# DeltaNet attention into a SiLU MLP: odd heads' copies and moves first, outputs stored in bundles, MLP steps and V's loads placed anew

## The chip, the core and the metric

The kernel runs on one core of a Trainium2 chip. Its time is the device time in microseconds (us). The core's engines are TensorE (PE; its weight loads are PEld), VectorE (DVE), ScalarE (ACT), GpSimd (POOL) and SyncE (SP), whose queue issues nearly all DMAs here. Each engine works through its own instructions in order; they wait for each other by semaphores.

## The reference

For 4 batches and 8 heads, over 768 tokens of 48 elements, a delta rule runs from token to token; its output, laid out as 3072 rows of 384, goes through an MLP with 2048 hidden units.

```python
k_n = k / (np.linalg.norm(k, axis=-1, keepdims=True) + 1e-06)
for t in range(S):
    kt, vt, bt = (k_n[:, :, t], v[:, :, t], beta[:, :, t, None])
    y[:, :, t] = np.einsum('bhd,bhde->bhe', q[:, :, t], state)
    v_old = np.einsum('bhde,bhd->bhe', state, kt)
    state = state + bt[:, :, :, None] * np.einsum('bhd,bhe->bhde', kt, vt - v_old)
...
x = y.transpose(0, 2, 1, 3).reshape(B * S, H * D)
h = x @ w_in
out = (h * (1.0 / (1.0 + np.exp(-h)))) @ w_out
```

## The kernel before

**Chunks.** The 768 tokens are cut into six chunks of 128 (c = 0 to 5), each into two halves of 64 tokens (hf = 0, 1). Batches come in two groups of two (g = 0, 1). Inside a chunk the delta rule is a triangular system per head. Its inverse is made in 32x32 blocks: `prepare` makes the scores of the next chunk on TensorE (`score`, L514) and sends their diagonal blocks to DRAM and back (`block_out`, `block_in`: "blocks", "g"), so that each of the 128 partitions holds one block. `invert` (L614) solves them on VectorE in 31 steps of two instructions (L625, L630), then scales the result (L633) and sends it out ("low", "up") and in again ("xe", "xi", "crossed").

**One chunk's solve** (L970) is a fixed chain on TensorE with evacuations between: merge (L780, into py), keys (L826), second merge (L780, into px), then for each half: inner products and old outputs together (L838, L904), `made` = update of the state (L858) and new outputs (L917), and between the halves keys again. `made` (L954) ends with `copy_out`, which runs `even_heads` (L925) for group 0; the next step of `solve` runs it for group 1 and then `move`.

**The way into the MLP.** `even_heads` copies the odd heads' rows of the output bank into "part" (one copy of 48x512), then the even heads' rows straight into xT (six copies). The odd heads' rows need other partitions, so five DMAs per half (`move`, L895; out L897) take them from "part" to xT, for both groups together. In chunk 1's first half group 1's copies are VectorE's (`by_dve`), else all are ScalarE's.

**The MLP** of a half is `feed_forward` (L1205), a chain of 30 steps: `hidden` (L1032) has 16, of three matmuls each (128x256 moving), with a SiLU on ScalarE after every second; `combine` (L1132) has 14, of four matmuls (128x192), in seven chains of eight matmuls. `combine` works with sums of weights and of hidden values, which VectorE makes (`sum_g`, L1128; the first sums of the three groups of hidden values stand at hidden steps 10 and 16 and at the first combine step). It writes the output tile "o" (one buffer) from the fourth combine step on (L1170, L1173, L1176 on ScalarE, L1157 on VectorE) and stores it at its end (`store`, L1057: four DMAs of 96 KB). Chunk 0's MLP uses `project` (L1062) instead, with eight bundles of projection matmuls (L1074) that lie beside chunk 1's solve. Every matmul stands in the trace as two records: a hidden step is 6 records, a combine step 8.

**The order of the work** is written out by hand. `pin` keeps each engine in program order, and `in_line` (L92) keeps SP's DMAs in order. A string per chunk (`chunks`, L1479) says what comes next: "s" one step of `solve`, "r" one step of the MLP (any pending chunk's), "y" one step of `prepare`, "g" the start of the next inversion, "i" one inversion step, "k" the loads of K, "m" a step of the key lengths. The string at L1543 does it for chunk 0 and the start of chunk 1 ("t" is a sum of weights, L1110, "z" a scaling of V, "f" a narrowing step of a weight, L229 to L249, "c" ends the projection). SP's order follows from that: in `solve`, `load_v(c + 1)` (L1013; eight DMAs, L198) stands behind the second half's inner products, `follow` loads the next q in blocks (twelve DMAs, L162).

Of the kernel before, what the change touches and what calls it, by code (L numbers as in the profile page):

```python
# [19 lines left out]
def kernel(  # L20
# [12 lines left out]
    DM, DFF = moe_w_in.shape  # L33
# [78 lines left out]
    def together(*parts):  # L112
        for _ in zip_longest(*parts):
            pass
# [223 lines left out]
    xis = [xi[:, g] for g in range(2)]  # L338
    crossed = const.tile([P, HH, T], FP32, name="crossed")

    def busy(n=1, after=None, how=NoSync):

        for _ in range(n):
            pw = bank(CC, "pw")
            done = pin(nc.tensor.matmul(
                pw[:, 0:DM], lhsT=ident[:],
                rhs=states[0][:].rearrange("p u a w -> p (u a w)")[:, 0:DM], start=True, stop=True,
            ))
            tensor.append(done.ins.engine)
            if after is not None:  # L350
                behind(done, after, how)
                after = None
# [572 lines left out]
    def even_heads(c, g, hf, py):  # L925

        xT, half = x_half(c, g, hf)
        if g == 0:
            parts[c, hf] = work.tile([P, 2, NP, C], FP32, name="part", tag="x", bufs=1)
        part = parts[c, hf][:, g]  # L930
        by = by_dve if c == 1 and hf == 0 and g == 1 else by_act
        by(part[0:D], py[0:D].rearrange("p (a t) -> p a t", a=NP))
        for h in chained(range(1, H, 2), range(0, H, 2)):
            f = D * h
            while f < D * (h + 1):
                n, at = min(D * (h + 1) - f, P - f % P), W * (1 - h % 2) + f - D * h
# [12 lines left out]
        yield  # L949
# [4 lines left out]
    def made(c, hf):  # L954

        together(update(c, 0, hf), update(c, 1, hf))
        together(new(c, 0, hf), new(c, 1, hf))
        copy_out()

    def follow(c):  # L960
# [9 lines left out]
    def solve(c):  # L970
# [31 lines left out]
        for hf in range(2):  # L1002
            if hf == 1:
                together(keys(c, 0, 1), keys(c, 1, 1))
                if c > 1:
                    follow(c)
                yield
            for g in range(2):
                together(inner(c, g, hf), old(c, g, hf))
            if hf == 1:  # L1010
                if c == 1:
                    follow(c)
                load_v(c + 1)  # L1013
            yield
            made(c, hf)
            yield
            copy_out()
            move()
            if hf == 0:
                yield  # L1020
# [11 lines left out]
    def hidden(c, hf):  # L1032

        for f in range(NFF // 2):
# [19 lines left out]
                    sum_g(which, f // FG - 1)  # L1054
            yield

    def store(c, hf, o, n, cols=slice(0, DM), two_queues=False):  # L1057
        for u in range(HB):
            row = (n * HB + u) * S + c * C + hf * W
            issue(out[row : row + W, cols], o[W * u : W * (u + 1), n, cols], two_queues and u == 1)  # L1060

    def project():  # L1062
# [6 lines left out]
        for f in range(NFF):  # L1069
            assert ("out", f // 2) in narrowed  # L1070
            for i in range(2 * HB):
                hf, n = i // HB, i % HB
                at = (f % 2) * GT + n * C
                pin(nc.tensor.matmul(  # L1074
                    pos[i][:, 0:DM], lhsT=hidden_of(0, hf, f // 2)[:, at : at + C],
                    rhs=w_outs[f // HFF][:, f % HFF, :], start=(f == 0), stop=(f == NFF - 1),
                ))
                if f == NFF - 1:
                    to = (o, rest)[hf]
                    pin(nc.scalar.mul(to[:, n], pos[i][:, 0:DM], 0.5))  # L1080
                    store(0, hf, to, n)
                if n == HB - 1 and (f < NFF - 1 or hf == 0):
                    yield
        A.append(rooms[0])
# [46 lines left out]

    def combine(c, hf):  # L1132

        o = mlp.tile([P, 2, DM], FP32, name="o", bufs=1)
        kept = mlp.tile([P, 3, HM], FP32, name="kept", bufs=1)
        px, py = bank(M, "px"), bank(M, "py")
# [61 lines left out]
        keep(2, py[:, left])  # L1198
        add(o[:, 0, right], kept[:, 2])
        add(o[:, 0, left], kept[:, 0])  # L1200
        for n in range(2):
            store(c, hf, o, n)
        yield

    def feed_forward(c, hf):  # L1205
# [220 lines left out]
    def prepare(c):  # L1426
# [50 lines left out]
    sums_made = sum_w()  # L1477
    later = {}
    chunks = {  # L1479
# [5 lines left out]
    }  # L1485

    def script(text):

        nonlocal pieces
        for word in text.split():  # L1490
# [25 lines left out]
                paced(load_q, 1)  # L1516
            elif what == "o":
                busy(n)
            elif what == "h":
                size_half(1, pins[seen_on])  # L1520
            elif what == "v":
# [6 lines left out]
                later["inv"] = invert(1, step)  # L1528
            elif what == "i":
                go(later["inv"], n)  # L1530
            elif what == "z":
                size(1, sizes_1.pop(0))
            elif what == "t":
# [6 lines left out]
                pieces = chained(feed_forward(1, 0), feed_forward(1, 1))  # L1540

    for text in (
        "s f3 s q q s j4 b j36 r j4 f j16 q f j4 f j16 r j44 b j4 q j4 r f r j22 f j12 f j8 f b j8 f j8 r j16 e r f j99 h f r f2 l s l r l p r l f p l s l2 f r3 l3 p l s l3 p l2 r l f l4 f l f l3 p l s l2 s2 f r f r p l3 g i p l p f i p f l i r3 i r v f i2 r3 i2 r i r i3 b r2 f2 r2 i r2 i2 r2 i f b i r i3 f2 r2 f r3 f i2 r f i f r3 f r f i f r i2 r i2 k i2 b r2 i r i r z r i r s r b z s b r2 t r2 f s r2 t2 m2 t2 b m f r m s f b r m r m2 b m f s r s m4 c s m7 r t s m r m5 s r m2 t2",  # L1543
    ):
        script(text)
    for c in range(1, NCH):
# [5 lines left out]
        for word in chunks[c].split():  # L1552
# [9 lines left out]
                inverse = invert(c + 1, step)  # L1562
            elif what == "i":
                go(inverse, n)
            elif what == "k":
                load_k(c + 2)
                if in_blocks(c + 2):
# [37 lines left out]
```

## Time and profile before

| | us |
|---|---|
| median of three runs | 650.05 |
| lowest and highest of them | 647.34, 651.13 |
| the profiled execution, its own time | 648.18 |
| span of that execution, first to last instruction | 646.2 |
| TensorE busy in it | 624.3 |
| VectorE, ScalarE, GpSimd busy | 398.0, 214.3, 91.0 |

The mean granted TensorE clock of that execution was 0.989. The profile is one execution; its time stands 1.87 us below the median. "Busy" counts an engine's instructions from start to end as the profile shows them; matmuls are pipelined and their ends modelled. An idle time is written with what ended it: "<-DMA xT<-part" means that the instruction waited for the DMA that writes xT from part; "issue" that the profile names nothing.

### The profile page before, as it was taken

The numbers are of one execution on the slowest core, as the hardware profiler recorded it, in microseconds if no ns is written. First come the engines' busy times: TensorE is split into PE (matmuls) and PEld (weight loads), VectorE is DVE, ScalarE is ACT, GpSimd is POOL, SyncE is SP. The second block draws the span as 40 slices with busy tenths as digits, with TensorE's granted clock in tenths as the row PEclk, the third lists the DMA queues.
The fourth block names the chain that finished last, engine by engine and source line by source line (L and its number), as shares of the span: only waits on it lengthen the run. The fifth ranks groups of instructions, "written<-read, shape, count | busy, mean of one in ns | idle before, by whom it ended". The sixth has DMA issues, their size and how long they took to land.

```text
span 646.2 us, 21378 instructions
## 1 busy us (share of the span) xinstructions
PE 624.3 (97%) x9406; PEld 546.1 (85%) x9406; DVE 398.0 (62%) x911; ACT 214.3 (33%) x497; POOL 91.0 (14%) x92
## 2 busy tenths in 40 slices
PE   7789999999999999999999999999999999999997
PEld 5478788666789988989988989989989989789997
DVE  5776889989765974554975454976454973102112
ACT  2456673441441122451122451122451122441111
POOL 5023721336020020010020010020011000000000
PEclk9969999999999999999999999999999999999999
DMA  9955833440479251359142259333163024100101
GB/s 138 212 144 174 257 81 88 116 81 3 98 133 156 52 91 19 84 113 160 39 91 36 66 121 160 57 78 45 38 144 71 20 66 50 40 13 1 25 0 25
DMA packets 145676, 54.70 MB, mean 85 GB/s; under 512 B 117152, under 2 KB 138912, under 8 KB 145584
## 3 DMA queue, kind: packets, MB, share of 16 engines
q1 hardware_dynamic: 143136, 52.93, 40.1%
q8 instruction: 74, 1.21, 0.8%
q10 hardware_dynamic: 2448, 0.41, 0.4%
q14 instruction: 18, 0.15, 0.1%
HBM read 40.14 MB, written 11.01 MB: 79 GB/s over the span
## 4 chain that ended last, share of the span: by engine, by line
PE 76%; DVE 11%; DMA 7%; SPq 2%; issue 2%; ACT 1%; ACTq 0%; POOL 0%; DVEq 0%; POOLq 0%
PE phid L1039 30%; PE px L1146 13%; PE py L1146 10%; PE po L1074 5%; DVE rank L625 4%; DVE x L630 3%; PE pb_c L838 3%; PE pa L527 2%; PE pb_c L826 2%; PE pb_c L1074 2%; PE pyc L917 1%; PE pb_c L858 1%; DMA up<-x 1%; DVE sums_of_g L1128 1%; PE pyc L904 1%
## 5 line engine op out<-in xcount | busy, mean ns | idle before, releaser
L1039 PE MATMUL phid<-xT,w_in 128*128 128x256 f32 x1152 | 258.4, 382 | 2.6 <-DMA xT<-part 1.3
L1039 PEld LDWEIGHTS phid<-xT,w_in 128*128 128x128 f32 x1152 | 215.9, 190 | 34.3 <-issue 4.3
L1049 ACT ACTIVATE gT<-phid 128x512 f32<-128x512 f32 x88 | 52.6, 597 | 144.8 <-PE phid L1039 131.5
L625 DVE SCALAR_TENSOR_TENSOR rank<-g,step,x 128x31 f32<-128x31 f32 (+15 forms) x124 | 49.7, 401 | 37.5 <-DMA g<-blocks 34.1
L1128 DVE TENSOR_TENSOR sums_of_g<-gT 128x384 f32<-128x384 f32 (+1 forms) x60 | 31.1, 538 | 57.3 <-ACT gT L1049 46.6
L1146 PE MATMUL py<-w_out,sums_of_g 128*128 128x192 f32 x320 | 56.8, 329 | 0.0
L1146 PE MATMUL px<-sums_of_w,sums_of_g 128*128 128x192 f32 x320 | 56.8, 329 | 0.0
L1146 PEld LDWEIGHTS px<-sums_of_w,sums_of_g 128*128 128x128 f32 x320 | 52.2, 190 | 0.5
L1146 PEld LDWEIGHTS py<-w_out,sums_of_g 128*128 128x128 f32 x320 | 52.2, 190 | 0.4
L630 DVE TENSOR_TENSOR x<-x,rank 128x31 f32<-128x31 f32 (+15 forms) x124 | 42.5, 343 | 4.3
L465 POOL TENSOR_TENSOR vf<-vf,n_slot 128x768 f32<-128x768 f32 x10 | 15.0, 1508 | 171.4 <-DMA vf<-in_v_dram 125.6
L486 DVE STREAM_TRANSPOSE kq<-stage 128x512 f32<-128x512 f32 x28 | 28.4, 1109 | 10.1 <-DMA stage<-in_q_dram 10.1
L542 ACT COPY xT<-pyc 48x128 f32<-48x128 f32 (+2 forms) x126 | 32.7, 260 | 1.6
L1146 PE MATMUL px<-sums_of_w,gT 128*128 128x192 f32 x160 | 28.4, 329 | 0.0
L1146 PE MATMUL py<-w_out,gT 128*128 128x192 f32 x160 | 28.4, 329 | 0.0
L1146 PE MATMUL px<-w_out,gT 128*128 128x192 f32 x160 | 28.0, 327 | 0.0
L1146 PEld LDWEIGHTS px<-w_out,gT 128*128 128x128 f32 x160 | 26.4, 190 | 0.5
L838 PEld LDWEIGHTS pb_c<-vf,xi 64*64 64x64 f32 x736 | 23.5, 138 | 4.0 <-issue 3.7
L548 POOL COPY g<-x 64x256 f32<-64x256 f32 x4 | 5.0, 1239 | 151.8 <-DVE x L633 151.8
L1146 PEld LDWEIGHTS py<-w_out,gT 128*128 128x128 f32 x160 | 26.1, 190 | 0.3
L1146 PEld LDWEIGHTS px<-sums_of_w,gT 128*128 128x128 f32 x160 | 26.1, 190 | 0.2
L1157 DVE TENSOR_TENSOR o<-o,kept 128x192 f32<-128x192 f32 (+1 forms) x29 | 11.5, 421 | 24.0 <-ACT kept L1154 24.0
(221 smaller groups left out, 920.7 us busy)
## 6 DMA issues: line engine op xcount, KB each, us to landing
vf<-in_v_dram SPq DMA_DIRECT2D x48, 96.0 KB, 3.0
out_dram<-o SPq DMA_DIRECT2D x42, 96.0 KB, 2.2
w_out<-in_moe_w_in_dram SPq DMA_DIRECT2D x4, 768.0 KB, 4.4
sums_of_w<-in_moe_w_out_dram SPq DMA_DIRECT2D x4, 768.0 KB, 4.5
blocks<-ap SPq DMA_DIRECT2D x44, 64.0 KB, 1.9
g<-blocks SPq DMA_DIRECT2D x5, 512.0 KB, 3.5
kb<-in_k_dram SPq DMA_DIRECT2D x12, 192.0 KB, 4.8
kb<-in_k_dram SPq DMA_DIRECT2D x24, 96.0 KB, 4.4
```

Of the source, the lines that this page charges most:

```text
L465: pin(nc.gpsimd.tensor_tensor(out=vf, in0=vf, in1=of, op=ALU.mult))
L486: pin(nc.vector.transpose(out=kqs[c, b][:, :, j, :].rearrange("p a (i m) -> p a m i", i=T), in_=src.rearrange("p a (m d) -> p a m d", d=D) ...
L527: pin(nc.tensor.matmul(pa[e][half, p * n * W : (p + 1) * n * W], lhsT=kq[rows, p, 0, half], rhs=kq[rows, p, js[0] : js[-1] + 1, half], sta ...
L542: return pin(nc.scalar.copy(to, of))
L625: pin(nc.vector.scalar_tensor_tensor(out=tv, in0=g[:, 0:m, m : m + 1].to_broadcast([P, m, n]), scalar=step[:, m : m + 1], in1=x[:, m : m + ...
L630: yield pin(nc.vector.tensor_tensor(out=x[:, 0:m, m:T], in0=x[:, 0:m, m:T], in1=tv, op=ALU.add))
L838: yield pin(nc.tensor.matmul(pz[rows, n * D : (n + 1) * D], lhsT=xis[g][rows, u * H + 2 * p + e, :], rhs=vfs[c][rows, hf, g * HB + u, p, : ...
L1039: pin(nc.tensor.matmul(ph[:, j * GT : (j + 1) * GT], lhsT=w_in[:, a, (2 * f + j) * P : (2 * f + j + 1) * P], rhs=xTs[c, hf][:, a, :], star ...
L1049: pin(nc.scalar.activation(out=hidden_of(c, hf, f), in_=ph[:], func=ACTF.Silu, scale=-0.5 if in_blocks(c) else 0.5))
L1074: pin(nc.tensor.matmul(pos[i][:, 0:DM], lhsT=hidden_of(0, hf, f // 2)[:, at : at + C], rhs=w_outs[f // HFF][:, f % HFF, :], start=(f == 0) ...
L1128: pin(nc.vector.tensor_tensor(out=sums_of_g[:, k, fs], in0=of[0], in1=of[1], op=op))
L1146: pin(nc.tensor.matmul(to, lhsT=at, rhs=quarter(f, *b) if isinstance(b, tuple) else sums_of_w[b][:, f], start=start and f == 0, stop=f == ...
```

## The change

1. `even_heads` yields between the odd heads' copy and the even heads' copies. `made` runs the first part for both groups, issues the moves at once, and copies group 0's even heads after that. Group 1's even heads come a step later, as before.
2. `combine` no longer stores its output at its end. It puts the two stores (four DMAs) on a list, `held`, and the next `combine` stores them at its start; a word "d" in a chunk's string does so earlier. The projection's first half is held as well.
3. `load_v(c + 1)` leaves `solve`; a word "v" (for chunk 2's V: "V") places it.
4. The strings of chunks 1 to 5 and the end of the first string place the MLP steps, inversion steps, stores and V's loads anew; the steps themselves stay.

The functions `busy` and the word "u" get a width that nothing uses.

```diff
         by(part[0:D], py[0:D].rearrange("p (a t) -> p a t", a=NP))
         for h in chained(range(1, H, 2), range(0, H, 2)):
+            if h == 0:
+                yield
             f = D * h
             while f < D * (h + 1):
...
         together(update(c, 0, hf), update(c, 1, hf))
         together(new(c, 0, hf), new(c, 1, hf))
+        for copy in copies:
+            next(copy)
+        move()
         copy_out()
...
                 if c == 1:
                     follow(c)
-                load_v(c + 1)
             yield
             made(c, hf)
...
             yield
 
+    held = []
+
+    def flush():
+        for stored in held:
+            store(*stored)
+        held.clear()
+
     def store(c, hf, o, n, cols=slice(0, DM), two_queues=False):
         for u in range(HB):
...
                     to = (o, rest)[hf]
                     pin(nc.scalar.mul(to[:, n], pos[i][:, 0:DM], 0.5))
-                    store(0, hf, to, n)
+                    if hf == 0:
+                        held.append((0, hf, to, n))
+                    else:
+                        store(0, hf, to, n)
                 if n == HB - 1 and (f < NFF - 1 or hf == 0):
                     yield
...
     def combine(c, hf):
 
+        flush()
         o = mlp.tile([P, 2, DM], FP32, name="o", bufs=1)
         kept = mlp.tile([P, 3, HM], FP32, name="kept", bufs=1)
...
         add(o[:, 0, right], kept[:, 2])
         add(o[:, 0, left], kept[:, 0])
-        for n in range(2):
-            store(c, hf, o, n)
+        held.extend((c, hf, o, n) for n in range(2))
         yield
...
     later = {}
     chunks = {
-        1: "s l99 y r2 g y r2 y r2 y r6 i r i r i r i k i r i r i r i2 r i r i r i2 r i r i r i2 r i r i r i2 r i r i r i3 r i r i2 r i r i r i2 r m4 r m4 r m4 r m4 r m4 r m4 r m4 r m4 m99",
-        2: "s r2 s r2 s r2 s r2 s r s r s r2 s r2 s r2 s y r2 g y r2 y r2 y r6 i r i r i r i k i r i r i r i2 r i r i r i2 r i r i r i2 r i r i r i2 r i r i r i3 r i r i2 r i r i r i2 r m4 r m4 r m4 r m4 r m4 r m4 r m4 r m4 r m4 r m4 m99",
-        3: "s r2 s r2 s r2 s r2 s r s r s r2 s r2 s r2 s y r2 g y r2 y r2 y r6 i r i r i r i k i r i r i r i2 r i r i r i2 r i r i r i2 r i r i r i2 r i r i r i3 r i r i2 r i r i r i2 r m4 r m4 r m4 r m4 r m4 r m4 r m4 r m4 r m4 r m4 m99",
-        4: "s r2 s r2 s r2 s r2 s r s r s r2 s r2 s r2 s y r2 g y r2 y r2 y r6 i r i r i r i k i r i r i r i2 r i r i r i2 r i r i r i2 r i r i r i2 r i r i r i3 r i r i2 r i r i r i2 r m4 r m4 r m4 r m4 r m4 r m4 r m4 r m4 r m4 r m4 m99",
-        5: "s r2 s r2 s r2 s r2 s r s r s r2 s r2 s r2 s",
+        1: "s l99 d y r3 g y2 r2 y r5 i r k i r i r2 i2 r i r i r i2 r i r i r i3 r3 i3 r i r i3 r i r i r i3 r i r i r i r i r i r i2 r m4 r m4 r m4 r m4 r m4 r m4 r m4 r m2 r m2 r m99",
+        2: "s r2 s r2 s r2 s r s r s2 r2 s r v d r2 s r2 s y r2 g r y2 r2 y r6 i r2 i2 r i k i r i r i r i2 r i r i r i2 r i r i r i2 r i r i r i2 r i r i r i3 r i r i2 r i r i r i2 m r m3 r m4 r m4 r m4 r m8 r m r m3 r m4 r m4 r m4 m99",
+        3: "s r4 s2 r2 s r2 s r s r s r2 s v r2 s r2 s d y r2 g y r2 y r2 y r7 i2 r i r i2 r i k r i r i2 r i r i2 r i r i r i r i2 r i r i r i2 r i r i r i3 r i r i2 r i r i3 r m4 r m r m3 r m4 r m4 r m3 r m5 r m4 r m4 r m4 r m4 m99",
+        4: "s r2 s r2 s r2 s r3 s r s r s r s r3 s2 d v y r3 g y r3 y r2 y r6 i r i2 r i2 r i r i2 r i2 r i r i r i2 r k i r2 i2 r i r i r i2 r i r i r i3 r i r i2 r i r i r i2 r m4 r m4 r m4 r m4 r m4 r m4 r m4 r m4 r m4 r m4 m99",
+        5: "s r2 s r s r2 s r2 s r s r s r2 s r s r2 s",
     }
...
             elif what == "i":
                 go(later["inv"], n)
+            elif what == "d":
+                flush()
+            elif what == "V":
+                load_v(2)
             elif what == "z":
                 size(1, sizes_1.pop(0))
...
 
     for text in (
-        "... i2 k i2 b r2 i r i r z r i r s r b z s b r2 t r2 f s r2 t2 m2 t2 b m f r m s f b r m r m2 b m f s r s m4 c s m7 r t s m r m5 s r m2 t2",
+        "... i2 k i2 b z r2 i r i r z r i r2 b r t r s r b r f s r2 t s t m2 t2 b m f r m s f b r m3 b m f s r2 s m2 c m2 s m7 r t s m r2 m5 s V r m2 t2",
     ):
         script(text)
...
             elif what == "i":
                 go(inverse, n)
+            elif what == "v":
+                load_v(c + 1)
+            elif what == "d":
+                flush()
             elif what == "k":
                 load_k(c + 2)
                 if in_blocks(c + 2):
```

More of the change, by code (lines that the diff above doesn't have):

```diff
@@ L339, with busy @@
     crossed = const.tile([P, HH, T], FP32, name="crossed")
-    def busy(n=1, after=None, how=NoSync):
+    NARROW = 160
+    def busy(n=1, after=None, how=NoSync, wide=DM):
         for _ in range(n):
@@ L345, in busy @@
             done = pin(nc.tensor.matmul(
-                pw[:, 0:DM], lhsT=ident[:],
-                rhs=states[0][:].rearrange("p u a w -> p (u a w)")[:, 0:DM], start=True, stop=True,
+                pw[:, 0:wide], lhsT=ident[:],
+                rhs=states[0][:].rearrange("p u a w -> p (u a w)")[:, 0:wide], start=True, stop=True,
             ))
@@ L1518, in script @@
                 busy(n)
+            elif what == "u":
+                busy(n, wide=NARROW)
             elif what == "h":
@@ L1542 @@
     for text in (
-        "s f3 s q q s j4 b j36 r j4 f j16 q f j4 f j16 r j44 b j4 q j4 r f r j22 f j12 f j8 f b j8 f j8 r j16 e r f j99 h f r f2 l s l r l p r l f p l s l2 f r3 l3 p l s l3 p l2 r l f l4 f l f l3 p l s l2 s2 f r f r p l3 g i p l p f i p f l i r3 i r v f i2 r3 i2 r i r i3 b r2 f2 r2 i r2 i2 r2 i f b i r i3 f2 r2 f r3 f i2 r f i f r3 f r f i f r i2 r i2 k i2 b r2 i r i r z r i r s r b z s b r2 t r2 f s r2 t2 m2 t2 b m f r m s f b r m r m2 b m f s r s m4 c s m7 r t s m r m5 s r m2 t2",
+        "s f3 s q q s j4 b j36 r j4 f j16 q f j4 f j16 r j44 b j4 q j4 r f r j22 f j12 f j8 f b j8 f j8 r j16 e r f j99 h f r f2 l s l r l p r l f p l s l2 f r3 l3 p l s l3 p l2 r l f l4 f l f l3 p l s l2 s2 f r f r p l3 g i p l p f i p f l i r3 i r v f i2 r3 i2 r i r i3 b r2 f2 r2 i r2 i2 r2 i f b i r i3 f2 r2 f r3 f i2 r f i f r3 f r f i f r i2 r i2 k i2 b z r2 i r i r z r i r2 b r t r s r b r f s r2 t s t m2 t2 b m f r m s f b r m3 b m f s r2 s m2 c m2 s m7 r t s m r2 m5 s V r m2 t2",
     ):
```

## The prediction

> **What bounds the kernel now.** I read the page's first part, then the busy time by stage (columns: stretch, length, then busy time of PE, PEld, DVE, ACT, POOL with counts), then TensorE's waits from 141 us on (total, times, longest).
>
> ```profile
> span 646.2 us, 21378 instructions
> ...
> PE 624.3 (97%) x9406; PEld 546.1 (85%) x9406; DVE 398.0 (62%) x911; ACT 214.3 (33%) x497; POOL 91.0 (14%) x92
> ```
> ```profile
> 0.00:94.00 94.00, 80.34 (x2144) 64.31 (x2145) 67.83 (x171) 52.32 (x110) 36.28 (x45) 0.93 0.73 170
> ...
> 168.00:189.00 21.00, 19.59 (x439) 16.53 (x441) 14.54 (x35) 9.04 (x27) 1.06 (x1) 1.00 0.71 146
> ...
> 240.00:275.00 35.00, 34.16 (x1017) 31.64 (x1017) 18.56 (x43) 12.79 (x36) 0.00 (x0) 1.00 0.36 59
> ...
> 300.00:340.00 40.00, 39.03 (x212) 36.25 (x211) 35.28 (x98) 6.93 (x14) 4.41 (x5) 1.00 0.46 82
> ...
> 531.00:570.00 39.00, 37.59 (x970) 33.56 (x969) 10.48 (x21) 13.04 (x36) 0.00 (x0) 1.00 0.27 42
> ...
> 624.00:646.20 22.20, 18.84 (x115) 18.47 (x114) 5.21 (x11) 2.42 (x6) 0.00 (x0) 1.00 0.08 18
> ```
> ```profile
> PE phid L1039 <- DMA xT<-part: 1.3, 2, 0.8
> PE py L780 <- DMA xe<-low: 1.3, 2, 1.0
> PE pb_c L838 <- issue: 0.7, 1, 0.7
> PE pb_c L826 <- issue: 0.6, 1, 0.6
> PE pa L527 <- DVE kq L486: 0.5, 1, 0.5
> ```
> TensorE is the bound: 624.3 of 646.2 us. Of its 21.9 us of idle time, 13.7 (94 − 80.34) lie in the first 94 us, which no edit reaches, and 3.4 (22.2 − 18.84) behind the last matmul. The four stretches between lack 1.4, 0.8, 1.0 and 1.4 us, 4.6 in all. No edit removes a matmul. So only those 4.6 us can be won, and what a change of work costs inside "busy" time:
>
> ```profile
> 250.69 2.80 PE py L1146 x16
> ...
> 590.92 2.60 PE py L1146 x16
> ...
> 603.92 20.72 PE phid L1039 x96
> ```
> In the chain of waits 16 combine records take 2.60 us among their like and 2.80 between attention groups: each return to MLP work costs 0.2. A combine step (8 records) is 1.30, a hidden step (6 records) 20.72 / 16 = 1.30 us.
>
> **The change part by part.**
>
> *Moves in the last chunk.* TensorE, ScalarE, the DMA queue, and the landing times of these moves:
>
> ```profile
> 559.46 0.67 PE L1039 MATMUL phid<-xT,w_in 128*128 128x256 f32 x2
> 560.67 0.67 PE L1039 MATMUL phid<-xT,w_in 128*128 128x256 f32 x2 [0.54 <-DMA xT<-part]
> 562.12 0.67 PE L1039 MATMUL phid<-xT,w_in 128*128 128x256 f32 x2 [0.78 <-DMA xT<-part]
> ```
> ```profile
> 554.15 0.58 ACT L542 COPY part<-pyc 48x512 f32<-48x512 f32 x1 [2.75 <-PE pyc L917]
> ...
> 556.61 0.57 ACT L542 COPY part<-pyc 48x512 f32<-48x512 f32 x1
> ```
> ```profile
> 557.20 3.37 SPq L897 DMA_DIRECT2D xT<-part  x5
> ```
> ```profile
> xT<-part SPq DMA_DIRECT2D x33, 48.0 KB, 2.1
> ```
> Two hidden records take 0.43 us, so the pairs at 560.67 and 562.12 came 0.78 and 1.02 late: 1.8 us, both xT waits of the list. The five moves wait for the second group's odd-head copy at 556.61, because the first group's even heads stand ahead of it. With both odd copies first they can start at 554.15 + 0.58 + 0.57 = 555.3, are issued by 558.7 and landed by 560.8. In the new order one combine step more and the 64 inner and old products stand ahead of this hidden step:
>
> ```profile
> 463.08 0.18 PE pb_c L838
> ...
> 465.11 2.79 PE phid L1039 x12
> ```
> Those products take 2.0 us (463.08 to 465.11, chunk 4), so the step starts at 559.46 + 1.30 + 2.0 = 562.8, 2.0 after the landing: **−1.8**. If the cover went, the old 1.8 would be back, so the ends are −1.8 and 0. In chunks 2 to 4 the same copies find no wait to remove; they only free the SP queue earlier.
>
> *Chunk 1.* Before, 38, 2, 8, 6, 4 and 6 projection matmuls stood between merge, keys, second merge, inner and update; now 44, 4, 4, 2, 2 and 8: as many ahead of the hidden step. On VectorE two narrowings (L238, L242) and one L1110 now precede the merge's copy.
>
> ```profile
> 145.21 1.02 DVE L831 TENSOR_TENSOR vf<-vf,pb_c 128x384 f32<-128x384 f32 x2 [1.43 <-issue]
> ...
> 146.74 0.96 DVE L242 SCALAR_TENSOR_TENSOR w_out<-sums_of_w,w_out 128x768 uint32<-128x768 uint32 x1
> ...
> 148.20 2.47 DVE L242 SCALAR_TENSOR_TENSOR w_out<-sums_of_g,w_out 128x768 uint32<-128x768 uint32 x1
> ```
> ```profile
> 167.06 2.48 SPq L106 DMA_DIRECT2D out_dram<-o  x4
> ```
> The second odd copy of this chunk is VectorE's (`by_dve`), so the five moves there follow VectorE's queue. The wait this adds at the hidden step is 0 if the narrowings fit into pauses like the 1.43 ahead of 145.21, and +1.4 if the first takes 2.47 like the second (2.47 − 0.96 = 1.5, rounded down). I take **+0.4**, nearer to the pause, in which VectorE stood idle just ahead of them. [...] Next, the projection's four stores (2.48 us of issue at 167.06) no longer stand ahead of q's loads, and one hidden step more stands ahead of the scores: the L486 wait of 0.5 goes, **−0.5** (ends −0.5 and 0). One return less here (the scores stand together) and one in chunk 3 (two combine pairs together): **−0.4**.
>
> *The merges of chunks 2 to 5* wait for the inversion: blocks out and in by DMA, some 30 us on VectorE, low and up out, xe in. SP's queue of chunk 2, then VectorE and xe's landing:
>
> ```profile
> 263.03 4.02 SPq L897 DMA_DIRECT2D xT<-part  x5
> 267.14 6.70 SPq L162 DMA_DIRECT2D stage<-in_q_dram  x12
> 274.03 6.22 SPq L198 DMA_DIRECT2D vf<-in_v_dram  x8
> 280.35 3.55 SPq L106 DMA_DIRECT2D out_dram<-o  x4
> 284.00 3.30 SPq L897 DMA_DIRECT2D xT<-part  x5
> 287.39 5.51 SPq L106 DMA_DIRECT2D blocks<-ap  x8
> ```
> ```profile
> 298.47 0.27 DVE L625 SCALAR_TENSOR_TENSOR rank<-g,step,x 128x31 f32<-128x31 f32 x1 [10.65 <-DMA g<-blocks]
> ...
> 299.47 0.55 DVE L1128 TENSOR_TENSOR sums_of_g<-gT 128x384 f32<-128x384 f32 x1
> ```
> ```profile
> DMA to landing us min/median/max: 2.2/3.2/4.2
> ```
> SP has no pause from 263 on: the blocks are late by the queue. In chunk 2 the four stores (3.55) go behind the blocks, so g lands up to 3.5 us sooner. But the L1128 sums need the 16th hidden step and now stand behind the first inversion step, where they stood behind the second: the chain cannot pass them, and the second step (0.5) moves behind them. So chunk 3's merge is ready 0.5 later against TensorE's work; its xe took the longest landing, 4.2, and the median is 1.0 less: **−0.5** of the 1.0 wait (ends −1.0 and +0.5). In chunk 3 it is the first step that moves behind the sums: chunk 4's merge, which is not among the waits above, waits **+0.2** (ends 0 and +0.5). Chunk 2's merge comes two combine steps later: its wait (1.3 − 1.0 = 0.3) goes, **−0.3** (ends −0.3 and 0). Chunk 5's stays at **0** (ends 0 and +1.3, since one combine step less stands between keys and the blocks there).
>
> *Stores and V.* A bundle is 2.5 us of issue, now at the next combine's start. The output tile is written again four combine steps (5.2 us) later:
>
> ```profile
> out_dram<-o SPq DMA_DIRECT2D x42, 96.0 KB, 2.2
> ```
> ```profile
> xi<-up SPq DMA_DIRECT2D x16, 128.0 KB, 3.9
> ```
> 2.5 + 2.2 = 4.7 fits if SP is free. In second halves it gets there only behind the xi loads, so ScalarE's L1170 may wait 1 to 2 us; TensorE needs that evacuation some 8 us after the merge: **0** (ends 0 and +0.7, in chunk 5, where two steps fewer cover it). [...] No row here has stores behind xi loads. V's eight loads stay ahead of the blocks, and its user on GpSimd is done before g lands: 0; with that cover gone it would cost what g's start loses.
>
> **Sum:** −1.8 + 0.4 − 0.5 − 0.4 − 0.5 + 0.2 − 0.3 = −2.9. The profiled execution took 648.18 us (span 646.2): 645.3. The median of three runs is 650.05, 1.9 above it; against that I predict **647.1**, 0.45% less. A measurement of this kernel tells about 0.5% (3.25 us) from no change.
>
> **Rivals.**
> (a) *All stalls go*: also the rest of chunk 3's wait (0.5), the new waits (0.6) and the two "issue" stalls (1.3), which have no named releaser and lie beside dense DMA traffic that the change thins. −2.9 − 2.4 = −5.3: 644.8, or 643 if the smaller "issue" stalls under 0.5 go too. Against it: nothing names their cause.
> (b) *The waits are passed on*: the moves gain 1.8 and the returns 0.4, but the merges and chunk 1 take their upper ends (+0.5 + 0.5 + 1.4) and the loads' gains 0.8 stay out or are taken back by chunk 5: −2.2 + 2.4 = +0.2 to −0.6 with them: about 649.8. For it: all four merges are within 1 us of their chain.
> (c) *Slower*: in chunks 1, 3 and 4 the bundle now stands directly ahead of the blocks, behind moves and V that wait for late data. If SP pauses there, the blocks go out one bundle (2.5 to 3.5 us) later. Chunk 2's merge has 2.5 us of new slack; chunks 4 and 5 have none and pay it whole: 5 to 7 us, less the 2.9: +2 to +4, 652 to 654. It decides from a pause of some 3 us in all. Against it: the number of issues ahead of the blocks is the same there, and q's loads start earlier.
>
> **Chances.** Forecast 0.46 (645.5 to 648.5; 0.20 of it beyond −0.5%), (a) 0.26, (b) 0.16, (c) 0.12 (0.09 beyond +0.5%). Faster 0.20 + 0.26 = 0.46; slower 0.09; same 0.45. The range takes in (a) down to 642 and (b) with the runs' own scatter up to 651.5; (c) is left out.
>
> **What would show it.** Right: no xT wait of TensorE in the last chunk and the five moves issued 1.5 us or more earlier against their update; no L486 wait; L1170 late after merges without a TensorE wait behind it; xe waits of TensorE under 1.3 us in all. Wrong: an xT wait at chunk 1's first hidden step over 1 us; xe waits over 2 us; SP idle ahead of the blocks; TensorE waiting for ScalarE at L1146.

## The result and the profile after

The changed kernel takes 644.84 us (median of 8 runs, 643.25 to 645.47) where the kernel before takes 648.73 beside it (8 runs, 646.71 to 651.13): ratio 0.9938, 95% interval 0.9917 to 0.9959. Timed again it was 645.97 against 649.97, ratio 0.9922 (0.9896 to 0.9948). So it gains 3.9 to 4.0 us by the medians; the forecast was 2.9. Its profiled execution took 645.05 us, where 645.3 was forecast. That these two stand so near is luck: the profile of before lies 1.87 us below its median and that of after 0.2 above its own, and what lies ahead of stage 1, which the change leaves alone, took 1.3 us more in after's profile (117.4 for 116.1, below).

First the head of the page of after and its busy time by stage, the answer to the two fences that open the prediction.

```profile
span 643.3 us, 21382 instructions
...
PE 624.3 (97%) x9406; PEld 547.9 (85%) x9406; DVE 396.3 (62%) x911; ACT 213.7 (33%) x497; POOL 90.0 (14%) x92
```
```profile
0.00:94.00 94.00, 81.80 (x2128) 65.38 (x2132) 67.83 (x172) 52.09 (x109) 36.25 (x45) 0.91 0.72 170
...
168.00:189.00 21.00, 19.29 (x457) 16.77 (x460) 14.07 (x33) 8.41 (x26) 0.00 (x0) 1.00 0.57 122
...
240.00:275.00 35.00, 34.76 (x1021) 32.08 (x1019) 19.76 (x51) 11.26 (x31) 0.00 (x0) 1.00 0.46 80
...
300.00:340.00 40.00, 40.00 (x329) 37.32 (x330) 35.25 (x100) 6.92 (x14) 4.42 (x5) 1.00 0.39 74
...
531.00:570.00 39.00, 38.51 (x975) 35.01 (x974) 9.88 (x20) 16.04 (x47) 0.00 (x0) 1.00 0.30 52
```

TensorE is as busy as before, 624.3 us. The four stretches that lacked 4.6 us now lack 1.71 + 0.24 + 0 + 0.49 = 2.4. TensorE's waits from 141 us on say which ones are left:

```profile
PE pb_c L840 <- issue: 1.2, 1, 1.2
PE pt L500 <- ACT xT L544: 0.5, 1, 0.5
PE pb_c L828 <- issue: 0.4, 2, 0.2
PE px L782 <- issue: 0.3, 1, 0.3
PE pyc L919 <- issue: 0.2, 1, 0.2
```

No wait for a DMA is left from 141 us on, and of the waits of before xT (1.3), xe (1.3) and kq (0.5) are gone. One new wait is there, the turns' (L500, 0.5). And "issue", 1.4 us before, is now 2.1 and most of the list.

Since a whole run scatters by some us, the work is compared by stages below. Stage c runs from the start of one run of seven combine chains to the next (in before: 201.06, 298.54, 395.98, 492.22, 585.56 us); stage 1 begins with the first projection matmul. Each is read from TensorE's records of one profile. "Before" and "after" have two profiles.

| kernel | ahead of stage 1 | 1 | 2 | 3 | 4 | 5 | sum of 1 to 5 |
|---|---|---|---|---|---|---|---|
| before | 116.1 | 84.9 | 97.5 | 97.4 | 96.2 | 93.3 | 469.4 |
| before, again | 117.7 | 85.8 | 97.1 | 97.0 | 96.2 | 93.7 | 469.8 |
| after | 117.4 | 84.9 | 96.3 | 95.8 | 96.1 | 92.0 | 465.2 |
| after, again | 119.1 | 84.6 | 96.4 | 95.8 | 96.0 | 92.0 | 464.8 |
| early moves alone | 117.2 | 86.3 | 96.3 | 96.0 | 96.5 | 92.9 | 468.1 |
| held stores alone | 119.9 | 85.7 | 97.8 | 96.0 | 96.2 | 92.9 | 468.7 |
| places alone | 117.5 | 85.1 | 96.2 | 98.1 | 100.4 | 91.2 | 471.0 |
| no early moves | 119.1 | 84.4 | 96.4 | 95.9 | 96.8 | 92.4 | 465.9 |
| no held stores | 117.4 | 85.1 | 96.0 | 96.3 | 96.4 | 91.1 | 464.9 |
| fewer fillers | 120.7 | 84.8 | 96.4 | 95.8 | 96.3 | 91.3 | 464.6 |
| 64 records more | 130.8 | 83.9 | 96.4 | 100.6 | 96.0 | 91.0 | 468.0 |
| two places shifted | 117.3 | 83.8 | 98.5 | 95.9 | 96.7 | 91.1 | 466.0 |
| and the scores | 118.3 | 89.6 | 99.0 | 96.2 | 96.2 | 91.2 | 472.2 |
| second halves held | 119.8 | 85.2 | 96.5 | 96.2 | 96.0 | 92.0 | 466.0 |

What lies behind stage 5 is 60.7 us in all of them. The change gains 4.3 us in stages 1 to 5 by the first profiles and 5.0 by the second. The first part, which it leaves alone, scatters from 116.1 to 119.9 us among the kernels that share it, more than the change is worth. In stages 2 and 3 the two profiles of after agree within 0.1 us and those of before differ by about 0.4. The second profiles were taken to see this: after's was expected within 0.3 us in each stage, and is; before's, expected within 0.3 in stages 2 to 5 if the order of the work rules, differs there by up to 0.5 and in stage 1 by 0.9, and its xe waits come to 2.0 us instead of 1.3, as was expected if the landing of DMAs rules.

### The profile page after: what moved, and what is told of

The parts are those of the page before. It is cut to its first block, busy times and chain, and to the rows that moved or that the text cites. A ratio compares the mean times of both kernels' runs of the same rounds, so it can differ in the third digit from the quotient of the medians.

```text
span 643.3 us, 21382 instructions
## 1 busy us (share of the span) xinstructions
PE 624.3 (97%) x9406; PEld 547.9 (85%) x9406; DVE 396.3 (62%) x911; ACT 213.7 (33%) x497; POOL 90.0 (14%) x92
## 3 DMA queue, kind: packets, MB, share of 16 engines
q8 instruction: 74, 1.21, 0.8%
## 4 chain that ended last, share of the span: by engine, by line
PE 92%; DVE 2%; DMA 2%; issue 1%; ACT 1%; SPq 0%; POOL 0%; ACTq 0%; DVEq 0%; POOLq 0%
PE phid L1045 38%; PE px L1163 17%; PE py L1163 13%; PE po L1087 5%; PE pb_c L840 3%; PE pa L529 2%; PE pb_c L828 2%; PE pb_c L1087 2%; PE pyc L919 2%; PE pb_c L860 1%; PE pyc L906 1%; PE px L782 1%; PE py L782 1%; PE pt L500 1%; PE pb_c L529 1%
## 5 line engine op out<-in xcount | busy, mean ns | idle before, releaser
L1144 DVE TENSOR_TENSOR sums_of_g<-gT 128x384 f32<-128x384 f32 (+1 forms) x60 | 29.7, 518 | 65.6 <-ACT gT L1055 55.2
L840 PEld LDWEIGHTS pb_c<-vf,xi 64*64 64x64 f32 x736 | 23.6, 138 | 4.4 <-issue 3.8
L865 DVE TENSOR_TENSOR state<-state,pb_c 128x384 f32<-128x384 f32 x22 | 11.2, 550 | 25.0 <-PE pb_c L860 24.9
L840 PE MATMUL pb_c<-vf,xi 64*64 64x48 f32 x736 | 25.3, 223 | 1.2 <-issue 1.2
```

The costliest lines, as they stand in the source:

```text
L840: yield pin(nc.tensor.matmul(pz[rows, n * D : (n + 1) * D], lhsT=xis[g][rows, u * H + 2 * p + e, :], rhs=vfs[c][rows, hf, g * HB + u, p, : ...
L1144: pin(nc.vector.tensor_tensor(out=sums_of_g[:, k, fs], in0=of[0], in1=of[1], op=op))
```

## The experiments

**One part of the change at a time.** The kernel before with only the early copies and moves:

```diff
             if h == 0:
+                yield
...
+        for copy in copies:
+            next(copy)
+        move()
         copy_out()
```

> The kernel before with only the odd heads' copies and the moves brought forward; strings and stores as before. A stage is the time from the start of one run of seven combine chains to the start of the next (before, chunk 5: 492.22 to 585.56, 93.3 us; after: 92.0). Theory A (the prediction's first term): the five moves of the last chunk are issued about 2 us earlier, the two xT waits (1.3 us) fall to 0.2 or less, chunk 5's stage gets 1.4 to 1.8 us shorter, the others stay within 0.3, the ratio is 0.997 to 0.998. Rival (the landing of the moves, not their issue, decides): 0.8 us or more of the xT waits stay, ratio 0.999 to 1.001.

Ratio 0.9976 (0.9958 to 0.9995). TensorE's waits from 141 us on:

```profile
...
PE phid L1044 <- DMA xT<-part: 0.5, 1, 0.5
PE py L780 <- DMA xe<-low: 0.5, 2, 0.3
PE pt L498 <- ACT xT L542: 0.4, 1, 0.4
...
```

Between the two theories: the wait in the last chunk falls from 1.3 to 0.5 (its hidden step 3.26 to 2.26 us), and not to 0. Stage 5 gets 0.4 to 0.8 us shorter. That the other stages stay was wrong: 2 and 3 get 0.8 to 1.4 us shorter, and stage 1 is 0.5 to 1.4 longer. The moves leave the queue earlier, and xe is waited for 0.5 us instead of 1.3 and 2.0 in the profiles of before. The turns' wait is there too.

Only the held stores:

```diff
     def combine(c, hf):
+        flush()
...
-        for n in range(2):
-            store(c, hf, o, n)
+        held.extend((c, hf, o, n) for n in range(2))
```

> The kernel before with only the bundles of stores held until the next combine starts; copies, moves and strings as before. Theory B (from the two traces: the four stores ahead of the blocks cost chunk 3's merge its wait): in chunk 2 the blocks go out 3 us sooner, low goes out 1 to 1.6 us sooner, the wait of 1.0 us for xe ahead of chunk 3's merge and the 0.4 inside it go, chunk 3's stage (97.4 before, 95.8 after) gets 1.0 to 1.4 shorter, ratio 0.998. Rival (the prediction's reason: the inversion cannot pass the sums behind the sixteenth hidden step): the blocks go out sooner, but low at most 0.5 us, and 0.5 us or more of the wait stay; ratio 0.999 to 1.0.

Ratio 0.999 (0.997 to 1.001). Theory B holds in its place, the third merge: low goes out 30.80 us behind the start of the chains instead of 32.46 and 32.06, and chunk 3's stage is 96.0. The other stages give nothing more; both xT waits of the last chunk stay (1.3).

Only the new strings and V's places (copies, moves and stores as before):

```diff
-            if h == 0:
-                yield
...
-        held.extend((c, hf, o, n) for n in range(2))
+        for n in range(2):
+            store(c, hf, o, n)
```

> The kernel after with copies, moves and stores as before: only the strings and V's places are new (the stores stand at each combine's end). Theory C (the places alone carry the last chunk too: its hidden step starts 2.6 us later against the moves): no xT wait of TensorE in the last chunk over 0.2 us, its stage 1.2 to 1.6 us shorter; chunk 2's stage 0.8 to 1.2 shorter, chunk 3's 0.2 to 1.0 shorter (the second merge's pair of combine steps stands together, but the bundles are ahead of the blocks again); ratio 0.995 to 0.997. Rival (the places gain only together with the early moves and the held stores): an xT wait of 0.8 us or more in the last chunk and an xe wait of 1 us or more ahead of a merge; ratio 0.998 or above.

Ratio 0.9965 (0.9948 to 0.9983). Waits and, around the longest, the stretches of TensorE (length, busy times; the granted clock is the third figure from the end):

```profile
PE phid L1040 <- DMA xT<-part: 2.0, 1, 2.0
PE py L782 <- DMA xe<-low: 1.8, 2, 1.3
...
```
```profile
460.00:469.30 9.30, 7.27 (x215) 6.28 (x214) 5.93 (x9) 4.75 (x16) 0.00 (x0) 1.00 0.21 47
469.30:474.00 4.70, 4.70 (x14) 3.68 (x14) 0.00 (x0) 0.60 (x1) 0.00 (x0) 0.64 1.07 180
474.00:480.00 6.00, 6.00 (x150) 5.30 (x148) 4.84 (x6) 3.69 (x12) 0.00 (x0) 1.00 0.56 122
```

Theory C is right on the last chunk: with the old copies its hidden step has no wait, so there the places alone do what the prediction gave to the moves. The rival is right elsewhere: 1.8 us of xe waits ahead of and in chunk 3's merge, and in chunk 4 the xT wait of 2.0, behind which TensorE runs at a clock of 0.64 for 4.7 us: 18 records of hidden steps take 8.03 us instead of 4.08. Places alone are 1.2 to 1.6 us slower than before in the stages of this one profile; by the times they are faster. This execution took 651.19 us, the longest of its kernel's, whose median is 648.45, so waits of 1.8 and 2.0 need not be there each time.

Everything but the early moves:

```diff
-            if h == 0:
-                yield
...
-        for copy in copies:
-            next(copy)
-        move()
         copy_out()
```

> The kernel after with copies and moves as before: strings, V's places and held stores stay. Theory C (the early moves are not needed beside the new places): as fast as the kernel after within 0.3 us, 644.5 to 645.3 by its median, ratio 0.993 to 0.995. Rival (the prediction, which gives the moves the 1.8 us): xT waits in the last chunk are back, 1 us or more, ratio 0.996 to 0.997.

Ratio 0.9964 (0.9939 to 0.9988), in the rival's range, but not for its reason: no xT wait is back in the last chunk. The stages sum to 465.9, 0.7 to 1.1 above after, mostly in chunk 4 (96.8; a hidden step there waits 0.16 for xT). Its runs scatter from 644.25 to 653.27, so the ratio settles little here.

Everything but the held stores:

```diff
...
-        held.extend((c, hf, o, n) for n in range(2))
+        for n in range(2):
+            store(c, hf, o, n)
```

> The kernel after with every bundle stored at its combine's end, as before; early moves, strings and V's places stay. With old stores and old moves the new places had an xe wait of 1.8 us ahead of and inside chunk 3's merge and an xT wait of 2.0 us in chunk 4. Theory F (the held stores are what chunk 3's merge needs in the new order): blocks of chunk 2 go out 5 us later against the hidden steps than in the kernel after, low 2.5 to 3 us later, chunk 3's stage 1.5 to 2.2 us longer (97.4 to 98.1 instead of 95.84), and chunk 4's xT wait smaller than 2.0 but there, 0.5 us or more; ratio to before 0.996 to 0.998. Rival (the early moves alone free SP enough): chunk 3's stage within 0.4 of 95.84, ratio 0.993.

Ratio 0.9944 (0.992 to 0.9968); stages 464.9, as in after. Theory F fell: low goes out 1.3 us later against the chains than in after (32.13 instead of 30.82), not 2.5 to 3, and the xe wait is 0.2. Beside the early moves the held stores gain 0.5 us in chunk 3 and nothing in all.

**The "issue" stalls.** Counted through TensorE's stream (weight loads, matmuls, semaphore events, in order of time), most of these stalls stand at numbers that come back from kernel to kernel, 194 or 195 past a multiple of 256:

```
number         1218   1475   4035   6339   6595   7874   16578  16835  11202
before         0.48   1.01   0.88   0.65   0.21   0.55   -      -      -
before again   0.94   0.86   1.13   1.56   0.76   -      -      -      -
after          0.35   0.88   0.87   1.24   -      0.24   0.17   0.33   -
after again    1.69   1.42   1.53   0.99   -      0.30   -      0.81   -
fewer fillers  3.60   0.88   -      -      1.15   -      -      -      -
64 more        -      3.42   -      -      -      -      -      -      1.50
```

Left out are one of 0.20 in after (5826) and one of 0.24 in the fewer fillers (5570), both 194 past. Not every "issue" time is of this kind: one of 0.4 to 0.7 us at the sums of the key lengths, about 35 us into the kernel, keeps to its work when the numbers are moved (186 past in before and after, number 954; at 1082 with 64 records more), and the 64 records more have one of 1.01 at number 1724, 188 past.

The trace also holds 74 packets of 16,384 bytes on an instruction queue (its number, q8, and 1.21 MB stand on the page), about one for 256 of the 18,958 instructions. In after the one that starts at 171.23 takes 1.42 us; the stall ends at 174.05, 1.40 behind it. The others of both kernels end 1.1 to 1.5 behind theirs. That reads as TensorE waiting for its code. To test it, two kernels move the numbers against the work. One has 5 filling matmuls fewer at the start (their results are used by nothing):

```diff
-    busy(4)
+    busy(1)
...
         first_queries(b)
-        busy(1)
-    PACKET, WINDOW = 256, 445
+    PACKET, WINDOW = 256, 425
```

> The kernel after with 5 of the filling matmuls of the first 25 us left out (10 records, 20 instructions of TensorE; they compute nothing that is used). The 'issue' stalls of TensorE stand in all six profiles at the same numbers of its instruction stream, 194 or 195 past a multiple of 256 (1218, 1475, 4035, 6339, 16578, 16835, ...), 1.2 to 1.5 us after a 16,384-byte packet of its instruction queue. Theory D (TensorE waits for its code, which comes in blocks of 256 instructions): the stalls stay at those numbers, so they move 20 instructions on in the work; the ones at 4035 and 6339 then come some 8 records of hidden step later and vanish (0.9 and 1.2 us), new ones may come elsewhere; stage of chunk 1 shorter by 1 us or more, ratio to before 0.990 to 0.993. Rival E (the work itself or the traffic beside it makes the stall): the last products of chunk 1's second half stall 0.6 to 1.6 us as before, the ratio stays at 0.994.

The other has 32 narrow ones more, whose results nothing uses either:

```diff
     busy(3)
+    busy(32, wide=16)
...
-    PACKET, WINDOW = 256, 445
+    PACKET, WINDOW = 256, 573
```

> The kernel after with 32 more filling matmuls of 16 columns at the start (64 records, 128 instructions, half a block of 256; what they compute is not used), and the early weight loads kept at the same work. Theory D: the stalls stay at the numbers 194 or 195 past a multiple of 256, so each falls 64 records earlier in the work: none at the last products of chunk 1's second half and none at the first hidden step of chunk 0's second half (0.9 to 1.5 us before), but others where 97 records of small matmuls stand ahead of such a number; the sum of the stalls changes by 1 us or more in either direction. Rival E: the same products stall as before, 64 records later in the stream.

Ratios 0.9962 (0.9942 to 0.9981) and 1.0172 (1.0142 to 1.0202). The longest wait of the fewer fillers from 90 us on, then that of the 64 records more:

```profile
PE pyc L919 <- issue: 1.2, 1, 1.2
...
```
```profile
PE px L782 <- issue: 1.5, 1, 1.5
...
```

The stalls at the last products of chunk 1's second half (L840) and at chunk 0's first hidden step behind its new outputs (number 4035) are gone in both, and others are there, at the same sort of number: 6595 in the one, 11202 in the other. That these stalls hang on the number in the stream, not on the work, is shown. That code is what they wait for is read from the packets. Theory D's gain did not come, because the first part lost it: with fewer fillers 3.6 us at number 1218, with the 64 records 10.4 us that the fillers themselves take (70 filling records run from 2.39 for 14.56 us, in after 6 for 4.21) and a stall of 3.4. Nor is the first part of the fewer fillers the same work at other numbers only: the mean granted clock of its profiled execution is 0.975, of after's 0.987. In stages 1 to 5 the fewer fillers are at 464.6, 0.2 to 0.6 below after; stage 1, for which theory D had at least 1 us less, is 84.8 for 84.9 and 84.6, since the stall at 6595 took the place of the one at 6339.

Two kernels try to use it by moving work past the numbers. One puts a step of the projection in the place of a hidden step in chunk 1, and a second combine step between keys and second merge in chunk 5:

```diff
-... s r2 s m2 c m2 s m7 r t s m r2 m5 s V ...
+... s r2 s m2 r m2 s c m7 t s m r3 m5 s V ...
-        5: "s r2 s r s r2 s r2 s r s r s r2 s r s r2 s",
+        5: "s r2 s r2 s r2 s r2 s r s r s r s r s r2 s",
```

> The kernel after with two places changed. In chunk 1's second half the last bundle of projection stands between keys and inner products, and the hidden step that stood there stands behind them: 6 records fewer ahead, so number 6339 of TensorE's stream falls 4 records into the hidden steps. In the last chunk two combine steps instead of one stand between keys and second merge, and one instead of two ahead of the last hidden step: number 16835 falls 8 records earlier in the second merge and its code is asked for beside slower work. Theory D (TensorE waits for code): the stall of 1.0 to 1.3 us at 6339 shrinks to 0.4 or less, the one of 0.3 to 0.8 at 16835 goes; stage of chunk 1 0.5 to 1.0 shorter than the 84.6 to 84.9 of the kernel after, chunk 5's 0.4 to 0.8 shorter than 92.0 unless an xT wait comes back; ratio to before 0.990 to 0.992. Rival E (the products themselves stall): 1.0 us or more remains there, ratio 0.993.

Ratio 0.9954 (0.9935 to 0.9973). Both stalls went, as theory D has it: stage 1 is 83.8, stage 5 91.1. Stage 2 pays 2.2 for it:

```profile
PE py L1163 <- DVE sums_of_g L1144: 1.7, 1, 1.7
...
```

The projection ends later, so its stores, q's loads and the blocks leave SP later (g is issued 1.9 us ahead of the chains instead of 3.8), and VectorE has the sums late.

The other moves two steps of scores in chunk 0 as well:

```diff
-... p l s l3 p l2 r l f l4 f l f l3 p l s l2 s2 f r f r p l3 g ...
+... p l s l3 l2 r l f l4 f l f l3 l s l2 s2 f r f r p p p l3 g ...
```

> As the kernel with those two places changed, and chunk 1's scores of 32 records that stood between the inner products of chunk 0's second half stand behind its new outputs: number 4035 falls 32 records later in the work, into hidden steps and scores. Theory D: the stall of 0.9 to 1.5 us at 4035 goes (0.2 or less), time 0.7 to 1.5 us below the kernel with the two places alone, ratio to before 0.988 to 0.991. Rival (the scores were covering the evacuation behind the inner products): a wait of 0.5 us or more for ScalarE at the inner products or the update of chunk 0, no gain.

Ratio 1.0062 (1.0034 to 1.0089). The stall at 4035 went, but stage 1 takes 89.6 us: chunk 1's first merge waits 3.2 us for VectorE (xe_y) and the projection 1.9 for a weight on GpSimd. Neither theory had that.

Last, held stores for second halves alone, the others at the combine's end:

```diff
-        held.extend((c, hf, o, n) for n in range(2))
+        for n in range(2):
+            if hf == 0:
+                store(c, hf, o, n)
+            else:
+                held.append((c, hf, o, n))
```

> The kernel after, with only the bundles of second halves (which stand ahead of the blocks) held; those of first halves go out at the combine's end, where SP is idle, instead of at the next combine's start, right at the merges. Theory D with traffic (code lands later while the bundle is being moved: 1.3 to 1.6 us a packet at chunk 5's merge in the kernel after, 1.2 with all stores at their old place): no 'issue' stall in chunk 5 over 0.2 us (0.5 to 0.8 in the kernel after), its stage 91.0 to 91.3 instead of 92.0; chunk 2's 95.9 to 96.2 instead of 96.3; chunk 3's at 95.84 as in the kernel after, since its blocks go out just as early; ratio to before 0.990 to 0.992. Rival (the bundles of first halves make no difference): stages as in the kernel after within 0.3, ratio 0.993.

Ratio 0.9928 (0.9902 to 0.9955): the rival, no difference from after beyond the interval; in its one profile the stages are within 0.3 us of after's but for chunk 3, which is 0.4 longer. The last chunk stalls as much (0.33 at 16835 again, stage 92.0) though no bundle goes out beside it, so the bundle is not needed for that stall. No version tried is faster than after beyond the intervals.

## Why the prediction was right, term by term

The size came out at 3.9 to 4.0 instead of 2.9. All its signs of being right are there (no xT wait in the last chunk, moves 2.0 us earlier, no L486 wait, xe waits under 1.3 us), and none of those against it is in after's two profiles. Yet two of its reasons do not stand, and that the size came so near is in part luck: the merges gave 2.1 us where 0.6 was forecast, and a cost of 0.4 did not come, while new stalls and a new wait, which it did not have, took 1.3 back in the first pair. The rows below are the named waits; small pauses inside the groups make up the rest of the stages.

| term | predicted | before to after, two profiles each |
|---|---|---|
| last chunk's xT wait | −1.8 | −1.8 (first hidden step 3.26, 3.24 to 1.49) |
| chunk 1's xT wait, VectorE's queue | +0.4 | 0 (hidden step 1.66 to 1.52) |
| wait for q's turn (L486) | −0.5 | −0.5 in one profile; in the other of before it is not there |
| two returns fewer | −0.4 | −0.4 |
| chunk 3's merge | −0.5 | −1.4, −0.9 |
| chunk 4's merge | +0.2 | −0.2, −0.1 |
| chunk 2's merge | −0.3 | −0.5, −0.9 |
| chunk 5's merge | 0 | 0, −0.9 |
| stores | 0 | 0 (no held stores: sums 464.9 and 465.0) |
| "issue" stalls | 0 | +0.8, −0.2 |
| not foreseen: turns wait for ScalarE | – | +0.5 |

*Last chunk.* Size and mechanism as forecast. ScalarE, the DMA queue and TensorE in after:

```profile
551.95 1.06 ACT L544 COPY part<-pyc 48x512 f32<-48x512 f32 x2 [1.46 <-PE pyc L919]
553.04 3.24 ACT L544 COPY xT<-pyc 48x128 f32<-48x128 f32 x12
```
```profile
553.04 14.48 SPq L899 DMA_DIRECT2D xT<-part  x10
```
```profile
560.51 1.56 PE L1045 MATMUL phid<-xT,w_in 128*128 128x256 f32 x6
```

The two odd copies run together and the moves (five of this half and five of the next stand in the one row) start at 553.04, 3.0 us behind the update (550.00), where they stood 5.0 behind it (557.20 and 552.19). The hidden step has no wait. But the cover was double: places alone take the whole wait, moves alone 1.0 of the 1.8. In chunk 4 the cover is double too: places alone have the xT wait of 2.0 there, but either the held stores (no early moves: 0.16) or the early moves (no held stores: stage 96.4) take nearly all of it.

*Chunk 1.* The narrowings went into VectorE's pauses, at no cost. In after they are:

```profile
143.51 0.96 DVE L242 SCALAR_TENSOR_TENSOR w_out<-sums_of_w,w_out 128x768 uint32<-128x768 uint32 x1
...
144.98 2.47 DVE L242 SCALAR_TENSOR_TENSOR w_out<-sums_of_g,w_out 128x768 uint32<-128x768 uint32 x1
```

The long one is as long as before, and as in before a step of GpSimd on the weight starts just ahead of it (144.70 for 1.93 us; in before 147.83 for 2.03, the long one at 148.20); that this step is what makes it long is not shown. But here the merge runs beside it (from 146.23) and its copy on VectorE comes behind it (148.35), and neither the next keys (150.22), the second merge (154.08) nor the hidden step wait for that.

*Merges.* Here the forecast was too small, by its own reason that the inversion steps stand behind the sums in VectorE's queue. SP in chunk 2, before and then after:

```profile
294.54 0.34 SPq L580 DMA_DIRECT2D g<-blocks  x1
...
331.00 0.45 SPq L106 DMA_DIRECT2D low<-g  x1
```
```profile
284.67 5.40 SPq L106 DMA_DIRECT2D blocks<-ap  x8
291.55 0.34 SPq L582 DMA_DIRECT2D g<-blocks  x1
...
329.49 0.50 SPq L106 DMA_DIRECT2D low<-g  x1
```

and VectorE, whose first step stood at 298.47 in before, before and then after:

```profile
300.53 0.30 DVE L625 SCALAR_TENSOR_TENSOR rank<-g,step,x 128x87 f32<-128x87 f32 x1
...
301.04 0.42 DVE L1128 TENSOR_TENSOR sums_of_g<-gT 128x256 f32<-128x256 f32 x1
```
```profile
295.47 0.26 DVE L627 SCALAR_TENSOR_TENSOR rank<-g,step,x 128x31 f32<-128x31 f32 x1 [7.51 <-DMA g<-blocks]
...
295.89 0.55 DVE L1144 TENSOR_TENSOR sums_of_g<-gT 128x384 f32<-128x384 f32 x1
...
297.52 0.31 DVE L627 SCALAR_TENSOR_TENSOR rank<-g,step,x 128x87 f32<-128x87 f32 x1
...
299.50 0.43 DVE L1144 TENSOR_TENSOR sums_of_g<-gT 128x256 f32<-128x256 f32 x1 [1.39 <-ACT gT L1055]
```

The step that failed: the sums that stand at the sixteenth hidden step (128x384) do not need it; at 295.89 they run without a wait. The ones that hold the chain are the next pair (128x256): they wait 1.39 us for ScalarE. The three inversion steps ahead of them (the third at 300.53 before, at 297.52 after) are now done by then. So the 3.1 us by which g comes sooner (4.0 to 7.1 ahead of the chains, which start at 298.54 and 298.67) give 1.6 us at low, where the prediction put +0.5. The floor is real, though: with g 8.4 ahead (fewer fillers) low again goes out 30.80 behind. The same misreading in small made chunk 4's +0.2 wrong: in chunk 3 the sums of 128x384 now run ahead of the first step (390.16) while VectorE waits for g, and with g only 0.1 us sooner low, which chunk 4's merge needs, is issued 1.0 sooner (33.15 to 32.19 behind the chains). Part of the rest is the profile chosen: before's second one waited more, also for its code at number 6339:

```profile
PE py L780 <- DMA xe<-low: 2.0, 3, 0.7
PE pb_c L838 <- issue: 1.6, 1, 1.6
...
```

Xe was waited for at three merges there, in chunks 2, 3 and 5. So the wait at chunk 5's merge is there in one profile of before and not in the other; after has no xe wait in either.

*Stores.* As forecast, ScalarE waits for the held bundle (its longest wait of this kind 5.7 us) and no TensorE wait stands behind it:

```profile
ACT o L1187 <- DMA out_dram<-o: 12.5, 3, 5.7
```
```profile
out_dram<-o SPq DMA_DIRECT2D x42, 96.0 KB, 2.5
```

The median landing of all stores, 2.5 us, does not tell how those behind the xi loads land. The bundles that stand directly behind such loads do (340 to 343 us in after, 536 to 540 in its second profile):

```profile
out_dram<-o SPq DMA_DIRECT2D x4, 96.0 KB, 3.2
```
```profile
out_dram<-o SPq DMA_DIRECT2D x4, 96.0 KB, 3.9
```

Ten such landings run from 2.2 to 4.2 us with a median of 3.4, nearer the 3.9 of the xi loads in before than the 2.2 of its stores. No run shows the +0.7 of the prediction's upper end all the same, because ScalarE had time: its evacuation (L1187) comes 0.7 to 1.8 us late in chunks 2 to 4. In chunk 5 it comes 5.4 us late, at 541.75, and the bank is written again 0.14 us behind the end of it (542.38): there is no wait, but nothing was left over.

*Turns.* Every profile with the early copies has a wait of 0.4 to 0.5 us in chunk 1's turns (L498, L500) for ScalarE's xT copies; none without them has it. Group 0's even heads now come one copy (0.57 us) later; that this is what holds the turns' bank is argued, not tried.

*Rivals.* (a) had the right time, 644.8, for half the right reason: every DMA wait from 141 us on went, but the "issue" stalls stayed, because they hang on the stream's numbers: the traffic did thin, from a DMA share of 0.71 to 0.57 in 168 to 189 us, and the stall there grew from 0.65 to 1.24. Its time was counted from 650.05, so that by the gain it had 5.3 where 3.9 to 4.0 came. (b) fell: no merge or hidden step took its upper end. (c) fell in after: SP does pause ahead of q's loads, from 362.20 to 364.40 and from 460.47 to 463.04, but the blocks go out no later against the chains (8.9 and 7.6 us ahead, in before 8.8 and 7.2). Its mechanism was near all the same: places alone take 4.2 us more than before in chunk 4, in the one profile, for one late transfer, by xT and not by the blocks.

## What to carry to other kernels

A wait that stands within a microsecond of its chain counts by its frequency (the xe waits of before came to 1.3 us in one profile and 2.0 in the other): take a second profile of the kernel before, and compare stages rather than whole runs. When a chain is said to be held by other work in its engine's queue, look up which data that work itself waits for (here 1.39 us for ScalarE); its place in the queue alone does not tell. Where "issue" stalls stand among small matmuls, count the instructions: here the numbers repeated, 194 or 195 past a multiple of 256, and work moved past 6339 and 16835 took the stalls there away. What the moved work released must be followed up before the gain is counted: stage 2 paid 2.2 us.

## What the runs showed of the hardware

The stalls at repeating numbers read as TensorE outrunning its own code where small matmuls stand close; that is an inference from the packets' times. In after's chunk 5 the packets of code start at 535.63, 539.32, 542.90 and 546.54, 3.6 us apart for 256 instructions (128 records); merge, two combine steps, keys, one step and merge, 344 records, take 1.22 + 2.80 + 1.08 + 1.50 + 1.22 = 7.8 us without a stall, 2.9 us for 128. The stalls at these numbers are 0.2 to 3.6 us long. The packet ahead of number 6339 takes 1.14 us in the first profile of before, and the stall there is 0.65; in the second the stall is 1.56, and why is open.

In two profiles a wait of TensorE was followed by a lower clock. Behind the wait of 2.03 us in chunk 4 of places alone the granted clock is 0.64 for 4.7 us, as shown above. Behind the stall of 1.50 us at number 11202 the granted clock is 0.61 in these 8 us, and the next two combine steps take 5.42 us instead of 2.80:

```profile
355.00:362.00 7.00, 5.50 (x202) 5.12 (x204) 1.14 (x3) 0.49 (x1) 0.00 (x0) 0.96 0.08 18
362.00:370.00 8.00, 8.00 (x170) 7.43 (x161) 3.38 (x6) 1.96 (x4) 0.00 (x0) 0.61 0.02 4
```

Behind the stall of 1.56 us in chunk 1 of before's second profile (ended at 174.37) it stays at 1.00, so that the wait is the cause is not shown.
